# A fused attention, MLP and mixture-of-experts kernel: where the routing table's fill is kept, and when it is sent

## The chip, the cores and the metric

The kernel runs on one core of a Trainium2 chip. A core has TensorE (matmuls), VectorE, ScalarE, GpSimd and SyncE, which here issues nearly all DMAs from one queue, in order. The metric is device time in microseconds; three runs of the kernel before took 1059.51, 1066.27 and 1064.67 us, with a median of 1064.67.

## What is computed

Three layers, one behind the other, all in float32 at the interface:

```python
scores = scale * q @ k.T                              # 4 x 8 heads, 576 x 576, head dimension 64
kth = the 32nd largest of each row; others are masked
attn = softmax(masked scores); x = attn @ v           # 2304 tokens x 512
h = x @ w_in; g = relu(h) + log1p(exp(-abs(h)))       # 512 -> 2048
x = g @ w_out                                         # 2048 -> 512
e = argmax(x @ w_gate); out = gate * (relu(x @ w1[e]) @ w2[e])   # one of 8 experts a token
```

w_in and w_out arrive as 64-bit numbers, whose bits are decoded on the chip.

## The kernel before

Part one does attention, the dense layer and the routing; part two the experts. The program is recorded in Python in an order with priorities, and a scheduler that plays a timeline of its own sets the order on each engine from it. So an edit that moves one instruction in that timeline can reorder others far behind it.

Attention goes over 16 pairs of heads (four batches, four pairs each). `prep_split` loads nothing itself: it takes qn, kn and vn, which `load` (L323) fetched, splits each into two halves of 16 bits (ScalarE L370, then a subtraction L371, on VectorE for the first pair and on GpSimd for later ones) and issues transposing DMAs for k (L373, into kt) and q (L376, into q1), copies of q1 into q2 (L377, L378) and six small DMAs for v (L388 to L390). The tiles kt, q1 and q2 are of the pool kv, the first that part one opens. Score matmuls (L456) go in groups of two tiles, 72 groups in all; each is followed by an exact search of the 32nd largest on VectorE (L496 to L522), the exponentials on ScalarE (L530, L532) with subtractions on GpSimd (L531, L541, L542), a transposing DMA of the probabilities (L544), and, three groups later, the matmuls with v (L559).

`decode` turns one piece of w_in or w_out (128 x 512 numbers) into float32: a DMA into w (L238), ScalarE L247 and L251, VectorE L249 and L252, GpSimd L253. For w_in `decode_w_in` then makes the two halves w_in_s (ScalarE L258 and L259, GpSimd L260). Two pieces are decoded at the start, and up to four a group later.

Units of one or two finished tiles of x go through the dense layer: `unit_x` splits x (ScalarE L606, GpSimd L607), transposes it by DMA (L608), then 16 steps of `layer1` (L646, with w_in_s) and `layer2` (L686, with w_out_s). `route` writes each token's row to `rows` and its number to `table`, at the place of its expert (an indirect DMA on GpSimd, L755). Places of the table that no token takes have to hold the number TRASH. `clear_table` writes it everywhere at the start: a GpSimd iota of 128 x 146 numbers in SBUF (L128), and a DMA of them to the table (L129). Part two reads the table (L932).

The fill's tile comes from a pool `fill` of its own, opened and closed inside `clear_table`, ahead of part one's pools, which are allocated where it was. `w_out_s` is a tile of 128 x 16 x 512 numbers in the pool wp of part one; its last block of 512 columns is written by the last pieces decoded of w_out.

Of the kernel before, what the change touches and what calls it, by code (L numbers as in the profile page):

```python
# [11 lines left out]
I32 = mybir.dt.int32  # L12
# [8 lines left out]
NT, DM, DFF = 2304, 512, 2048  # L21
E, F2 = 8, 1024
# [3 lines left out]
KF = DFF // 128  # L26
KF2 = F2 // 128
SLOT = 256
# [7 lines left out]
TRASH = NT  # L36
# [58 lines left out]
def attn_moe_moe2(ctx, tc, q, k, v, w_in, w_out, w_gate, w1, w2, out):  # L95
    nc = tc.nc
# [11 lines left out]
                            fill=0.0, base=0, channel_multiplier=-1)  # L108
# [13 lines left out]
    table = dram.tile([E * NT + SLOT, 1], I32, name="table")  # L122
    rows = dram.tile([NT + 1, ROWW], F32, name="rows")

    def clear_table():
        with tc.tile_pool(name="fill", bufs=1) as p:
            fill = p.tile([128, (E * NT + SLOT) // 128], I32, name="fill")
            nc.gpsimd.iota(fill, pattern=[[0, (E * NT + SLOT) // 128]], base=TRASH, channel_multiplier=0)  # L128
            nc.sync.dma_start(table.rearrange("(p a) o -> p (a o)", p=128), fill)  # L129

    zrow = const.tile([27, 19], F32, name="zrow")
    nc.vector.memset(zrow, 0.0)
    nc.sync.dma_start(rows[TRASH:TRASH + 1, :].rearrange("o (p a) -> (o p) a", a=19), zrow)
# [2 lines left out]
    for i in range(2):  # L136
        h = ids[64 * i:64 * i + 64]
        nc.gpsimd.iota(h[:, :4 * B].rearrange("p (b t) -> p b t", t=4), pattern=[[S, B], [2, 4]], base=i,
                       channel_multiplier=R)
# [36 lines left out]

    def run(halves):
        nc.vector.memset(done, 0.0)
        clear_table()
        with ExitStack() as p:  # L180
            late = part_one(tc, p, q, k, v, w_in, w_out, const, ident, before, ones, iota_e, reg_e, wg, ids,
                            ohcum, done, early, table, rows, flags if halves else None, sums, w_sums, e_sums, kths)
        args = w1, w2, out, ident, ones, ohcum, done, early, late, table, rows, meta, left, rare
        with ExitStack() as p:
            part_two(tc, p, *args, (check, again) if halves else None, True)

        rv = nc.values_load(rare[0:1, 0:1], min_val=0, max_val=256)
        with tc.If(rv > 0):
            with ExitStack() as p:
                part_two(tc, p, *args, None, False)  # L190
            if halves:

                fv = nc.values_load(again[0:1, 0:1], min_val=0, max_val=128)
                with tc.If(fv > 0):
                    nc.vector.memset(ohcum, 0.0)
                    run(False)

    run(True)


def part_one(tc, ctx, q, k, v, w_in, w_out, const, ident, before, ones, iota_e, reg_e, wg, ids,
             ohcum, done, early, table, rows, flags, sums, w_sums, e_sums, kths):
    nc = tc.nc
# [24 lines left out]
    w_out_s = wp.tile([128, KF, DM], F32, name="w_out_s")  # L228
# [44 lines left out]
    def all_sum(bd, pool, tag):  # L273

        n = bd.shape[1]
        pb = pool.tile([128, 512], F32, name=tag)
        nc.tensor.matmul(pb[:, 0:n], lhsT=ones, rhs=bd, start=True, stop=True)
        bb = sm.tile([128, n], F32, name="bb" + tag)
        nc.vector.tensor_scalar(bb, pb[:, 0:n], 1e-30, None, op0=ALU.max)
        return bb  # L280

    w_inv = wp.tile([128, DFF // C], F32, name="w_inv")

    def split_w_in(j):
        bd = sm.tile([128, KD], F32, name="bdw")
        for kk in range(KD):
            t = dec.tile([128, C], F32, name="t")
            nc.scalar.activation(t, w_in_f[:, kk, j], AF.Abs, accum_out=bd[:, kk:kk + 1])
        bs = sm.tile([128, 1], F32, name="bs")
        nc.vector.tensor_reduce(bs, bd, op=ALU.add, axis=AX.X)  # L290
        up, down = pow2(all_sum(bs, ps_h, "h"), "h")
        nc.vector.tensor_scalar(w_inv[:, j:j + 1], down, 2.0 ** -8, None, op0=ALU.mult)
        for kk in range(KD):
            t = dec.tile([128, C], F32, name="t")
            nc.scalar.activation(t, w_in_f[:, kk, j], AF.Copy, scale=up)
            nc.scalar.activation(w_in_s[:, kk, j, 0], t, AF.Copy)
            nc.gpsimd.tensor_tensor(out=w_in_s[:, kk, j, 1], in0=t, in1=w_in_s[:, kk, j, 0], op=ALU.subtract)
# [11 lines left out]
    def decode_some(n):  # L309
        for _ in range(n):  # L310
            if dec_q:
                f, *a = dec_q.pop(0)
                f(*a)
# [12 lines left out]
    def prep_load(m):  # L326
        src = [None] * 3
        bd = sm.tile([128, 3], F32, name="bd") if flags is None else sums[:, m]
        pair[m] = (src, bd)
        for i in range(3):  # L330
            load(m, i)
        if flags is None:
            magnitudes(m, stg.tile([128, R * D], F16, name="st"))
# [6 lines left out]
    def prep_scale(m):  # L340
        b = pairs[m][0]
        src, bd = pair[m]
        if flags is not None:
            return
        up, iv = pow2(all_sum(bd, ps_m, "m"), "m")
        sc = sm.tile([128, 8], F32, name="sc", bufs=KVB + 2)
        nc.vector.tensor_copy(sc[:, 0:3], up)
        nc.vector.tensor_tensor(out=v_up[:, b:b + 1], in0=v_up[:, b:b + 1], in1=up[:, 2:3], op=ALU.min)
        nc.vector.scalar_tensor_tensor(sc[:, 3:4], iv[:, 0:1], 1.0 / D ** 0.5, iv[:, 1:2],
                                       op0=ALU.mult, op1=ALU.mult)  # L350
        nc.vector.tensor_scalar(sc[:, 4:5], sc[:, 3:4], -1.0, None, op0=ALU.mult)
        for i in (1, 0, 2):
            nc.scalar.activation(src[i], src[i], AF.Copy, scale=sc[:, i:i + 1])
        pair[m] = (*src, sc)
# [106 lines left out]
    def emit_scores(gi):  # L461
        s = row.tile([128, 2, S], F32, name="s")
        pa = ps_s.tile([128, 2, PS], F32, name="sa")
        for i, x in enumerate(groups[gi]):
            emit_qk(*x, pa[:, i], 0, 4)
        nc.scalar.activation(s[:, :, :PS], pa, AF.Copy)
        pb = ps_s.tile([128, 2, 512], F32, name="sb")
        for i, x in enumerate(groups[gi]):
            emit_qk(*x, pb[:, i, :PS + US], 4, R)
        if flags is None:  # L470
            nc.scalar.activation(s[:, :, PS:], pb[:, :, :PS + US], AF.Copy)
        sc_t[gi] = s, pb
# [224 lines left out]
    def some_work(k):  # L697
        for _ in range(k):
            moe_step()
            if side:  # L700
                next(side[0], None)
                if side[0].gi_frame is None:
                    side.pop(0)
# [144 lines left out]
    for i in range(-1, n + LAG):  # L848
        if i == -1:
            with tc.high_priority(offset=AHEAD):  # L850
                for m in range(RB):
                    prep_load(m)
                prep_scale(0)
        for m, step in steps.get(i, []):
            with tc.high_priority(offset=A_PREP):
                prep_step(m, step)
        while done_prep < whole and when[done_prep] <= i:
            with tc.high_priority(offset=A_PREP):
                if to_scale:
                    prep_scale(to_scale.pop()[0])  # L860
                prep_split(done_prep)
                if done_prep + RB < len(pairs):
                    prep_load(done_prep + RB)
                if done_prep + 1 < len(pairs):
                    to_scale.append((done_prep + 1, i + SCALE))
            done_prep += 1
        if to_scale and to_scale[0][1] <= i:
            with tc.high_priority(offset=AHEAD):
                prep_scale(to_scale.pop()[0])
        if i == -1:  # L870
            decode_some(2)
        if i + 1 < n:
            with tc.high_priority(offset=A_SC):
                emit_scores(i + 1)
        if 0 <= i < n:
            with tc.high_priority(offset=AHEAD):
                emit_softmax(i)
            with tc.high_priority(offset=0):
                decode_some(DECR)
        j = i - LAG  # L880
        if j >= 0:
            with tc.high_priority(offset=A_AV), ExitStack() as behind_scores:
                if i + 1 < n:

                    behind_scores.enter_context(tc.issue_after(last_qk[0].ins))
                for x in groups[j]:
                    emit_av(*x)
            for u in units.get(j, []):
                started += 1
                ready.append((u, started))  # L890
        if ready or cur or behind or side:
            credit += MOER
            some_work(int(credit))
            credit -= int(credit)
# [270 lines left out]
```

## Time and profile before

| | |
|---|---|
| three runs | 1059.51, 1066.27, 1064.67 us |
| the profiled execution, device time | 1059.72 us |
| its span in the profile | 1058.0 us |
| TensorE busy | 885.0 us, 84% |
| VectorE busy | 849.3 us, 80% |
| ScalarE busy | 801.2 us, 76% |
| GpSimd busy | 604.0 us, 57% |
| mean granted clock of TensorE | 0.936 of full speed |
| the hardware DMA queue's packets | 67.1% of 16 engines' span |

The span runs from the first to the last instruction of one execution; its device time is 1.7 us longer. Busy time is an average over stages with different limits: attention and the dense layer run interleaved up to about 740 us, the experts behind that. An engine's idle time costs something only where others wait for it, so a stage is read by what its engines waited for.

### The profile page before, as it was taken

Reading aid. Unit: us, or ns where it says so; the run is one execution under the profiler, and the core shown is the slowest. Engines: PE = TensorE matmul, PEld = TensorE weight load, DVE = VectorE, ACT = ScalarE, POOL = GpSimd, SP = SyncE. Lnnn points to the kernel's source line nnn. Section 1 sums busy time; section 2 is a strip of 40 time slices with the busy share of each in tenths; the row PEclk is TensorE's granted clock in tenths of the full one; section 3 lists DMA queues with packets and bytes.
Section 4 is the critical chain, followed back from the end, with each engine's and each line's share of the span. In section 5 each row is a group of like instructions: output and inputs, shape, how many; then the busy total and the mean of one; then the engine's idle time right before and its main releaser. Section 6 shows DMA issues by size and latency. Waiting matters only on the chain.

```text
span 1058.0 us, 22206 instructions
## 1 busy us (share of the span) xinstructions
PE 885.0 (84%) x7146; PEld 655.0 (62%) x7146; DVE 849.3 (80%) x3021; ACT 801.2 (76%) x1866; POOL 604.0 (57%) x631
## 2 busy tenths in 40 slices
PE   1124359774998989998999999999999999999994
PEld 0013236443675656675666666676787989999993
DVE  4779999998997968996989999955356987777773
ACT  5878898988888979987998888863678555555552
POOL 3888898998767768876778777652001022111111
PEclk9986559876999989998999999999999999999998
DMA  7897799788799987669978855464301667666650
GB/s 188 193 205 189 180 192 193 179 168 172 114 131 164 138 152 129 117 80 150 152 131 120 99 90 95 72 86 131 102 12 31 170 220 243 242 212 230 237 202 23
DMA packets 295859, 156.97 MB, mean 148 GB/s; under 512 B 257524, under 2 KB 257652, under 8 KB 295732
## 3 DMA queue, kind: packets, MB, share of 16 engines
q1 hardware_dynamic: 292116, 145.73, 67.1%
q0 software_dynamic: 3616, 9.72, 2.6%
q8 instruction: 58, 0.95, 0.4%
q14 instruction: 69, 0.57, 0.2%
HBM read 77.89 MB, written 11.11 MB: 84 GB/s over the span
## 4 chain that ended last, share of the span: by engine, by line
PE 47%; DVE 13%; DMA 12%; ACT 9%; POOL 8%; issue 6%; SPq 4%; POOLq 0%; ACTq 0%; DVEq 0%
PE h L646 11%; PE h L996 9%; PE y L686 8%; PE y L1009 8%; PE y L683 3%; DVE mx L522 3%; DVE wk L518 3%; DMA xT<-xh 3%; POOL e L531 2%; POOL p L542 2%; DMA w<-in_moe_w_in_dram 2%; PE sb L456 2%; PE m L559 1%; ACT e L532 1%; PE sa L456 1%
## 5 line engine op out<-in xcount | busy, mean ns | idle before, releaser
L646 PE MATMUL h<-xT,w_in_s 128*128 128x256 f16 (+1 forms) x1920 | 228.7, 269 | 22.9 <-ACT sa L660 14.4
L686 PE MATMUL y<-w_out_s,g 128*128 128x512 f32 x480 | 229.0, 601 | 1.3 <-ACT g L661 1.2
L646 PEld LDWEIGHTS <-w_in_s 128*128 128x128 f16 x1920 | 174.9, 101 | 82.7 <-issue 52.7
L531 POOL TENSOR_TENSOR e<-s,e 128x576 f32<-128x576 f32 x144 | 204.0, 1432 | 17.7 <-ACT e L530 10.4
L522 DVE MAX8 mx<-wk 128x8 f32<-128x128 f32 (+2 forms) x432 | 200.9, 503 | 0.1
L542 POOL TENSOR_TENSOR p<-e,p 128x512 f16<-128x512 f32 x144 | 167.8, 1165 | 0.0
L456 PEld LDWEIGHTS <-q 128*128 128x128 f16 (+1 forms) x640 | 55.8, 108 | 175.4 <-issue 125.8
L518 DVE MATCH_REPLACE8 wk<-mx,wk 128x128 f32<-128x128 f32 (+1 forms) x432 | 145.1, 343 | 0.1
L686 PEld LDWEIGHTS y<-w_out_s,g 128*128 128x128 f32 x480 | 82.7, 192 | 64.0 <-issue 58.1
L976 POOL DMA_INDIRECT out_dram<-ot,idx x19 | 19.5, 1028 | 176.1 <-DVE ot L975 173.4
L532 ACT ACTIVATE e<-e,bias 128x576 f32<-128x576 f32 x144 | 110.4, 768 | 12.7 <-POOL e L531 12.2
L996 PEld LDWEIGHTS h<-xT,wf 128*128 128x128 f32 x864 | 111.8, 191 | 5.4 <-ACT wf L957 0.2
L996 PE MATMUL h<-xT,wf 128*128 128x256 f32 x864 | 113.9, 283 | 0.0
L456 PE MATMUL sa<-kt,q 128*128 128x256 f16 (+1 forms) x320 | 54.0, 302 | 71.0 <-DMA kt<-st 23.4
L1009 PE MATMUL y<-wf,hT 128*128 128x512 f32 x432 | 112.8, 398 | 0.0
L456 PE MATMUL sb<-kt,q 128*128 128x320 f16 (+1 forms) x320 | 62.7, 338 | 53.6 <-ACT s L502 53.5
L530 ACT ACTIVATE e<-s,kths 128x576 f32<-128x576 f32 x144 | 104.9, 767 | 0.8
L559 PEld LDWEIGHTS <-pT 128*128 128x128 f16 (+1 forms) x1440 | 86.8, 106 | 22.9 <-issue 19.8
L559 PE MATMUL m<-v,pT 128*128 128x65 f16 (+1 forms) x1440 | 93.9, 201 | 7.2 <-DVE xtail L586 4.3
L540 ACT ACTIVATE p<-e 128x576 f16<-128x576 f32 x144 | 97.4, 678 | 0.7
L541 POOL TENSOR_TENSOR p<-e,p 128x64 f16<-128x64 f32 x144 | 46.1, 320 | 70.4 <-ACT p L540 65.9
L1009 PEld LDWEIGHTS y<-wf,hT 128*128 128x128 f32 x432 | 76.7, 189 | 13.0
(235 smaller groups left out, 1791.1 us busy)
## 6 DMA issues: line engine op xcount, KB each, us to landing
w1r<-in_moe_w_dram SPq DMA_DIRECT2D x20, 1024.0 KB, 6.3
w2r<-in_moe_w_dram SPq DMA_DIRECT2D x20, 1024.0 KB, 7.8
w<-in_moe_w_in_dram SPq DMA_DIRECT2D x16, 512.0 KB, 4.0
w<-in_moe_w_out_dram SPq DMA_DIRECT2D x16, 512.0 KB, 4.0
rows<-xr SPq DMA_DIRECT2D x37, 128.2 KB, 3.1
qn<-in_q_dram SPq DMA_DIRECT2D x16, 288.0 KB, 4.1
kn<-in_k_dram SPq DMA_DIRECT2D x16, 288.0 KB, 6.1
vn<-in_v_dram SPq DMA_DIRECT2D x16, 288.0 KB, 3.5
```

Source lines behind the costliest of these rows:

```text
L456: last_qk[0] = nc.tensor.matmul(ps[p0:p1], lhsT=qs[:, h, r0:r1, :].rearrange("p r d -> p (r d)"), rhs=kt[:, k0:k1, cs], start=first, stop= ...
L518: nc.vector.match_replace(out=to, in_to_replace=mx[:, i, 8 * j:8 * j + 8], in_values=src[i], imm_value=NEG)
L522: nc.vector.max(out=mx[:, i, 8 * j + 8:8 * j + 16], in_=src[i])
L530: nc.scalar.activation(e[i], s[i], AF.Relu, bias=kths[:, 2 * gi + i], scale=-K_UP)
L531: nc.gpsimd.tensor_tensor(out=e[i], in0=s[i], in1=e[i], op=ALU.subtract)
L532: nc.scalar.activation(e[i], e[i], AF.Exp, bias=bt[:, i], scale=SCORE)
L542: nc.gpsimd.tensor_tensor(out=p16[:, S + D:], in0=e[i][:, 0:S - D], in1=p16[:, 0:S - D], op=ALU.subtract)
L559: nc.tensor.matmul(o[:, h, 0:D + 1], lhsT=pT(r), rhs=v16[:, h, c, 0:D + 1], start=r == 0, stop=r == R - 1)
L646: nc.tensor.matmul(hps[:, :n], lhsT=w_in_s[:, c, j, p, o:o + 128], rhs=xT[:, 0:len(u.tiles), r, c, :], start=m == 0, stop=m == 3 * KD - 1)
L686: nc.tensor.matmul(u.y[i], lhsT=g[:, cs], rhs=w_out_s[:, f, :], start=f == 0, stop=f == KF - 1)
L996: nc.tensor.matmul(h, lhsT=w1f[:, a, c, :], rhs=xT[:, b, c, :], start=n == 0, stop=n == 3 * KD - 1)
L1009: nc.tensor.matmul(y[i], lhsT=hT[g][:, a, i * 128:i * 128 + 128], rhs=w2f[:, b, :], start=g == 0 and n == 0, stop=g == KF2 - 1 and n == 2)
```

## The change

The function `clear_table` moves into part one. Its tile is now the first 146 numbers of the last block of `w_out_s`, read as integers, and it is called behind the first pair's preparation and the first two decoded pieces, in place of the call ahead of part one. Nothing else is edited.

```diff
-    def clear_table():
-        with tc.tile_pool(name="fill", bufs=1) as p:
-            fill = p.tile([128, (E * NT + SLOT) // 128], I32, name="fill")
-            nc.gpsimd.iota(fill, pattern=[[0, (E * NT + SLOT) // 128]], base=TRASH, channel_multiplier=0)
-            nc.sync.dma_start(table.rearrange("(p a) o -> p (a o)", p=128), fill)
...
     def run(halves):
         nc.vector.memset(done, 0.0)
-        clear_table()
         with ExitStack() as p:
             late = part_one(tc, p, q, k, v, w_in, w_out, const, ident, before, ones, iota_e, reg_e, wg, ids,
...
+    def clear_table():
+        fill = w_out_s[:, KF - 1, :(E * NT + SLOT) // 128].bitcast(I32)
+        nc.gpsimd.iota(fill, pattern=[[0, (E * NT + SLOT) // 128]], base=TRASH, channel_multiplier=0)
+        nc.sync.dma_start(table.rearrange("(p a) o -> p (a o)", p=128), fill)
...
         if i == -1:
             decode_some(2)
+            clear_table()
         if i + 1 < n:
             with tc.high_priority(offset=A_SC):
                 emit_scores(i + 1)
```

The scheduler's order changes with it, on all engines. In the changed kernel line numbers up to here are 2 to 7 lower (L374 is what L376 was), and the numbers behind names differ. SP's queue near its start, before; q_170 is the first pair's q1, p_177 its split input, fill the table's fill:

```order
L133 DMA rows<-zrow 27x19
L129 DMA table<-fill 128x146
L238 DMA w<-in_moe_w_in_dram 128x1024 x2
L323 DMA qn<-in_q_dram 128x576
L376 DMA_TRANSPOSE q_170<-p_177 128x9x64
L373 DMA_TRANSPOSE kt<-st 128x9x128
L376 DMA_TRANSPOSE q_170<-p_177 128x9x64
L388 DMA v_184<-vs 64x5x130
L377 DMA q_171<-q_170 64x1152
```

And now, q_163 being the first pair's q1:

```order
L127 DMA rows<-zrow 27x19
L231 DMA w<-in_moe_w_in_dram 128x1024 x2
L278 DMA table<-w_out_s 128x146
L374 DMA_TRANSPOSE q_163<-p_170 128x9x64
L371 DMA_TRANSPOSE kt<-st 128x9x128
L374 DMA_TRANSPOSE q_163<-p_170 128x9x64
L386 DMA v_177<-vs 64x5x130
L375 DMA q_164<-q_163 64x1152
```

The table's DMA went behind the two loads of w_in, and a load of qn (of the second pair) is gone from here. SP's queue a little further on, from the first pair's copy of q, before (q_205 is the second pair's q1; the loads of qn, kn and vn are the third pair's and the second pair's):

```order
L378 DMA q_171<-q_170 64x1152
L376 DMA_TRANSPOSE q_205<-p_215 128x9x64 x2
L389 DMA v_184<-vs 64x4x130
L390 DMA v_184<-vs 64x130
L388 DMA v_184<-vs 64x5x130
L389 DMA v_184<-vs 64x4x130
L390 DMA v_184<-vs 64x130
L323 DMA qn<-in_q_dram 128x576
L323 DMA kn<-in_k_dram 128x576
L323 DMA vn<-in_v_dram 128x576
L238 DMA w<-in_moe_w_in_dram 128x1024 x2
L377 DMA q_206<-q_205 64x1152
```

And now, where q_198 is the second pair's q1 and the three loads are all the second pair's:

```order
L376 DMA q_164<-q_163 64x1152
L387 DMA v_177<-vs 64x4x130
L388 DMA v_177<-vs 64x130
L386 DMA v_177<-vs 64x5x130
L387 DMA v_177<-vs 64x4x130
L388 DMA v_177<-vs 64x130
L321 DMA qn<-in_q_dram 128x576
L321 DMA kn<-in_k_dram 128x576
L321 DMA vn<-in_v_dram 128x576
L231 DMA w<-in_moe_w_in_dram 128x1024 x2
L374 DMA_TRANSPOSE q_198<-p_208 128x9x64 x2
L371 DMA_TRANSPOSE kt<-st 128x9x128
```

The second pair's two transposes of q went behind the loads of kn, vn and w_in. GpSimd's queue at the first unit's split of x (x_778), before:

```order
L253 TENSOR_TENSOR w_out_s<-xr,w 128x512
L419 TENSOR_TENSOR st<-qn,st 128x9x64
L531 TENSOR_TENSOR e<-s,e 128x576 x2
L607 TENSOR_TENSOR xh<-x_778,xh 128x512
L253 TENSOR_TENSOR t<-xr,w 128x512
```

And now, the same tile being x_773:

```order
L539 TENSOR_TENSOR p_1333<-e,p_1333 128x64
L540 TENSOR_TENSOR p_1333<-e,p_1333 128x512
L417 TENSOR_TENSOR st<-qn,st 128x9x64
L605 TENSOR_TENSOR xh<-x_773,xh 128x512
L529 TENSOR_TENSOR e<-s,e 128x576 x2
```

The split of x went ahead of the two subtractions of the group's softmax.

## Rows read from the trace of the kernel before

**Rows 1.** The page: span; engine, busy us, share, instructions.
```profile
span 1058.0 us, 22206 instructions
PE 885.0 (84%) x7146; PEld 655.0 (62%) x7146; DVE 849.3 (80%) x3021; ACT 801.2 (76%) x1866; POOL 604.0 (57%) x631
```

**Rows 2.** Stretches: length, busy us of each engine (instructions), clock, DMA share, GB/s.
```profile
0.00:60.00 60.00, 9.50 (x34) 4.27 (x34) 39.39 (x127) 42.67 (x87) 36.55 (x49) 1.00 0.83 195
...
200.00:300.00 100.00, 71.01 (x641) 48.04 (x640) 93.20 (x335) 88.04 (x194) 87.58 (x91) 0.80 0.85 154
...
500.00:600.00 100.00, 97.96 (x894) 66.91 (x893) 93.30 (x383) 90.34 (x217) 78.40 (x85) 1.00 0.87 129
...
900.00:1000.00 100.00, 100.00 (x652) 91.29 (x651) 71.03 (x119) 56.54 (x112) 15.94 (x16) 1.00 0.64 223
```

**Rows 3.** Timeline of SP's queue: start us, us, line, operation, out<-in, count.
```profile
3.20 0.37 SPq L129 DMA_DIRECT2D table<-fill  x1
3.61 0.93 SPq L238 DMA_DIRECT2D w<-in_moe_w_in_dram  x2
...
7.43 1.34 SPq L376 DMA_TRANSPOSE q<-p  x1
8.87 1.87 SPq L373 DMA_TRANSPOSE kt<-st  x1
10.79 1.28 SPq L376 DMA_TRANSPOSE q<-p  x1
...
14.07 0.49 SPq L377 DMA_DIRECT2D q<-q  x1
...
15.29 2.59 SPq L376 DMA_TRANSPOSE q<-p  x2
...
21.88 0.42 SPq L323 DMA_DIRECT2D kn<-in_k_dram  x1
...
22.87 0.85 SPq L238 DMA_DIRECT2D w<-in_moe_w_in_dram  x2
```

**Rows 4.** Waits of SP's queue, 0 to 50 us: total us, times, longest.
```profile
SPq L376 <- DMA table<-fill: 1.9, 1, 1.9
```

**Rows 5.** Timeline of VectorE; in brackets idle time before, and its releaser.
```profile
4.35 0.76 DVE L371 TENSOR_TENSOR p<-qn,p 128x576 f16<-128x576 f32 x1 [2.45 <-ACT p L370]
...
30.55 0.70 DVE L249 TENSOR_SCALAR y<-y 128x512 uint32<-128x512 uint32 x1 [1.97 <-ACT y L247]
...
36.74 0.43 DVE L496 TENSOR_TENSOR sb<-sb,s 128x256 f32<-128x256 f32 x1 [0.37 <-ACT s L466]
```

**Rows 6.** Timeline of ScalarE: two reads of loaded pieces of w_in.
```profile
9.41 0.62 ACT L247 ACTIVATE y<-w 128x512 f32<-128x512 f32 x1 [1.95 <-DMA w<-in_moe_w_in_dram]
...
29.90 0.62 ACT L247 ACTIVATE y<-w 128x512 f32<-128x512 f32 x1 [2.05 <-DMA w<-in_moe_w_in_dram]
```

**Rows 7.** Timeline of TensorE: first scores of the first and second pair.
```profile
13.36 0.37 PE L456 MATMUL sa<-kt,q 128*128 128x256 f16 x1 [13.36 <-DMA kt<-st]
...
33.59 1.01 PE L456 MATMUL sa<-kt,q 128*128 128x256 f16 x4 [10.09 <-DMA kt<-st]
```

**Rows 8.** Stretches of one microsecond, columns as in rows 2.
```profile
8.00:9.00 1.00, 0.00 (x0) 0.00 (x0) 0.00 (x0) 0.00 (x0) 0.00 (x0) 1.00 0.93 363
```

**Rows 9.** The chain that ended last: start us, us, what (second unit's x).
```profile
261.64 3.09 DMA xT<-xh
```

**Rows 10.** All instructions of line L530: duration min/median/max ns, first and last start.
```profile
L530 ACT ACTIVATE e<-s,kths x144: 757/763/801, 32.2 to 699.4; 128x576 f32<-128x576 f32 x144
```

**Rows 11.** Waits, 200 to 220 us, on decoded pieces of w_in.
```profile
PEld L646 <- ACT w_in_s L259: 7.0, 2, 4.9
PE h L646 <- ACT w_in_s L259: 6.4, 2, 4.4
```

**Rows 12.** Timeline of GpSimd at the first unit's split of x.
```profile
143.48 1.59 POOL L531 TENSOR_TENSOR e<-s,e 128x576 f32<-128x576 f32 x1
145.04 1.60 POOL L607 TENSOR_TENSOR xh<-x,xh 128x512 f16<-128x512 f32 x1
```

## The prediction

> **What bounds the kernel now.** I read four views in this order: the table of stretches, the timelines of the first 40 us engine by engine, the list of SP's waits, and the chain of work that ended last. The page gives a span of 1058.0 us and TensorE busy for 885.0 us of it [rows 1]. The stretches show where its 173 idle us lie [rows 2]: in the first 60 us TensorE works 9.5 us, from 200 to 300 us it works 71.0 of 100, from 500 to 600 it works 98.0, from 900 to 1000 it works 100. So the kernel has two regimes. Up to some 260 us attention sets the pace: from 200 to 300 us VectorE is busy 93 of 100 us and ScalarE and GpSimd 88 each. Behind that TensorE is the bound, and its work is the same before and after. What the change can do is to bring the second regime forward or push it back, and whatever it moves there should reach the end.
>
> The change touches the first microseconds. The timeline of SP shows its DMAs there [rows 3]: table<-fill at 3.20, two loads of w_in from 3.61, then the first transpose, of q, at 7.43. VectorE had that transpose's input ready at 4.35 + 0.76 = 5.11 [rows 5], yet SP stood still for 1.9 us, and the list of its waits names table<-fill as the releaser [rows 4]. The transposed tile is the first one of the pool that was opened where the fill's pool had been closed, so it takes over the fill's bytes and has to wait until the DMA that reads them has landed. Everything of the first pair stands behind that transpose in SP's queue: kt at 8.87, the second half of q at 10.79, the copy of q at 14.07 [rows 3]; TensorE's first matmul follows at 13.36, released by kt [rows 7].
>
> **The change part by part.** (1) The fill moves to the last columns of w_out's place. GpSimd's iota keeps its place in the order and its size. The bytes that it borrows are decoded into only at the end of the weights, long after the table has been written, and the first scatter into the table needs a routed unit; so the new place adds a wait that nothing reaches. Price nothing; the cover is the whole of part one's first two sweeps.
>
> (2) The wait of the first transpose goes. In the changed order SP issues the two loads of w_in, then the table, then the transpose. The issues take 0.93 and 0.37 us [rows 3], so 3.20 + 0.93 + 0.37 is 4.5, and the transpose then waits for VectorE alone, to 5.11. It starts 7.43 - 5.11 = 2.3 us earlier. kt's input is the next VectorE row, so kt and the second half of q can follow back to back as they do now, and with them the scores of the first pair. The bound above is 2.3 us. The bound below is nothing: the transposes are now issued while two pieces of w_in are still under way. ScalarE got the first of it at 9.41, having waited for it 1.95 us [rows 6], and from 8 to 9 us the DMA engines moved 363 GB/s with a share of 0.93 [rows 8], so there is no free room for transposes before some 9 us. I take 2.3 of it, since kt, the late one, was issued at 8.87 and landed at 13.36: there is room behind 9.4 us that the three transposes can fill more densely than one after the other from 7.43 to 12.07.
>
> The Trainium skill (DMA: Bandwidth & Descriptors, section Queues, rings and completion order) speaks against this step: SP has one row of rings, and on each DMA engine descriptors are consumed in ring order, so a transpose behind the loads of w_in is served after them. No row of this case separates the service of a transpose from its landing; by that rule alone the step would give what the first rival below gives.
>
> (3) The second pair's loads move in SP's queue, since the schedule is made anew. Before, qn of the second pair was issued ahead of the first transpose and its two transposes stood at 15.29 for 2.59 us, ahead of kn at 21.88 and w_in at 22.87 [rows 3]. Now kn and w_in stand ahead of these two transposes, and qn behind the first pair's work. kn is therefore issued 2.6 + 2.3 = 4.9 us earlier, at 17.0, and w_in at 18.0. Before, the way from kn's issue to the second pair's scores on TensorE took 33.59 - 21.88 = 11.7 us [rows 3, 7]. Now the two transposes of 2.6 us fall into that way, so the scores come at 17.0 + 11.7 + 2.6 = 31.3, again 2.3 us earlier. The earlier w_in has an effect of its own: ScalarE waited 2.05 us for that load at 29.90 and VectorE 1.97 us behind it [rows 5, 6], and these waits can go, which would make it 2.3 + 2.0 = 4.3 us on VectorE. But at 36.74 VectorE already waited 0.37 us for the second pair's scores [rows 5], so what it gains there it waits for here. In the sum this is nothing; the bounds are nothing and 2.0 us.
>
> (4) The order behind that differs in many places. At the first unit GpSimd now splits its x ahead of the next group's two subtractions, the second of which took 1.59 us right before it [rows 12]; the unit can start some 3.2 us earlier. That is hidden, since TensorE is not the bound there: the second unit's x was transposed only at 261.64 [rows 9]. The decoding of weights is put off by up to a group against the softmax and meets it again by the second unit: the work up to there is the same, and its price is nothing while TensorE idles 29 of 100 us [rows 2].
>
> The sum: 2.3 + 0 + 0 = 2.3 us less. Against the profiled execution, 1059.72 us, that is 1057.4. The three runs shown have a median of 1064.67 and reach from 1059.51 to 1066.27, so the profiled one is a fast one; the mean of the four is 1062.5, and against that I forecast 1060 us.
>
> **Rivals.** *The transposes wait in the DMA engines instead.* They are issued early and served late, so the change does not do what it says: no gain, 1062.5 us. For it speaks the full share at 8 to 9 us [rows 8]; against it that the new order has one load less ahead of the transposes, the second pair's qn.
>
> *The new order gains a group.* Attention goes ahead of decoding. 144 rows of the softmax's first step, two a group, lie between 32.2 and 699.4 us [rows 10], so a group takes 667 / 71 = 9.4 us. If unit two starts one group earlier and TensorE then stays full, the gain is 9.4 + 2.3 = 11.7, 1051 us. Against it: the second unit's split moves by less than a group in GpSimd's order, and the decoding has been made up by then.
>
> *The late decoding holds up TensorE, and the kernel gets slower.* TensorE already waited for the last decoded parts of w_in, 6.4 us and its weight loads 7.0 us between 200 and 220 us [rows 11]; in the new order the first unit's last four steps stand one group later. TensorE works its queue in order, so scores behind these steps come late, VectorE starves, and one group is lost: 9.4 - 2.3 = 7.1 us more, 1069.6 us. It decides when that wait grows past the idle time around it, that is when the last matmuls of the first unit push the scores behind them by more than the 2.3 us won. Against it: the second unit could not begin before 261.64 + 3.1 [rows 9], so the first has from 220 to 264.7 us, some 45 us, to end.
>
> **How the numbers follow.** I give the forecast 0.45, the first rival 0.20, the second 0.20, the third 0.15. What a measurement of this kernel can tell from no change is about 1%, 10.6 us. Only the second rival comes to it, and just so: faster by over 1% 0.16, half of that rival and 0.06 of the spread of the others. Slower by over 1% 0.09: 0.05 for the third rival with a second group lost, and the spread of the others. Within 1%: 0.75. The range leaves out the far halves of the second and third rivals: 1050 to 1069 us. For the likeliest case alone it is 1056 to 1063: 4.3 to no gain, and the scatter of the runs.
>
> **What would show it.** In the changed profile SP's first transpose should start at 5.1 to 5.3 us and no longer be released by a DMA of the table; TensorE's first matmul should come at 11 us and the second pair's scores at 31. If the first matmul is still at 13, the DMA engines held it. If unit two's x is transposed at 252, the second rival is right; if the wait for w_in of rows 11 doubles and the unit's x comes after 262, the third. The forecast is wrong if the second regime begins at another time by more than 5 us, or if TensorE's idle time behind 300 us changes.

## The result

The changed kernel takes 1067.42 us (median of 20 runs, 1062.07 to 1072.5), the kernel before 1060.12 (20 runs, 1053.61 to 1066.27): a ratio of 1.0058, 95% interval 1.0041 to 1.0074. It is slower by 0.6%, some 6 us by the ratio and 7.3 us by the medians, where 2.5 us less was forecast. The profiled execution took 1062.07 us and is the fastest of its twenty, so a second profile of the same kernel, with 1074.82 us, stands beside it below.

The page of the kernel after, and its stretches, answer [rows 1, 2]:

```profile
span 1060.4 us, 22234 instructions
PE 884.7 (83%) x7146; PEld 653.7 (62%) x7146; DVE 854.3 (81%) x3021; ACT 801.3 (76%) x1866; POOL 603.8 (57%) x631
```

```profile
0.00:60.00 60.00, 9.89 (x37) 4.60 (x38) 40.97 (x130) 46.08 (x96) 39.85 (x52) 1.00 0.84 201
200.00:300.00 100.00, 72.28 (x639) 48.06 (x638) 92.75 (x331) 86.80 (x193) 88.44 (x89) 0.77 0.76 150
500.00:600.00 100.00, 97.33 (x854) 65.43 (x853) 90.19 (x367) 87.64 (x208) 75.95 (x82) 0.99 0.81 129
```

TensorE's work is the same 885 us; it does more of it by 60 and by 300 us, and less from 500 to 600. At the start the lead that was forecast is there, in part smaller and in part larger. SP's timeline, answering [rows 3]:

```profile
3.21 0.83 SPq L231 DMA_DIRECT2D w<-in_moe_w_in_dram  x2
4.09 0.43 SPq L278 DMA_DIRECT2D table<-w_out_s  x1
5.17 1.33 SPq L374 DMA_TRANSPOSE q<-p  x1
6.61 2.55 SPq L371 DMA_TRANSPOSE kt<-st  x1
...
17.61 0.42 SPq L321 DMA_DIRECT2D kn<-in_k_dram  x1
```

TensorE's first scores of both pairs, answering [rows 7]:

```profile
11.75 0.37 PE L454 MATMUL sa<-kt,q 128*128 128x256 f16 x1 [11.75 <-DMA kt<-st]
...
29.11 0.37 PE L454 MATMUL sa<-kt,q 128*128 128x256 f16 x1 [5.85 <-DMA kt<-st]
```

The first transpose starts at 5.17 instead of 7.43, the first matmul at 11.75 instead of 13.36, the second pair's scores at 29.11 instead of 33.59. The wait for decoded parts of w_in did not grow: 6.5 us on the weight loads from 100 to 260 us, against 7.0 before.

```profile
PEld L644 <- ACT w_in_s L252: 6.5, 3, 3.1
```

The second unit's x, in the chain that ended last, is at 259.56 instead of 261.64 [rows 9]. The same chain holds the row on which the result turns:

```profile
259.56 3.67 DMA xT<-xh
...
485.74 9.28 DMA xT<-xh
```

To see where the lead goes, take the dense layer's steps (ScalarE's `sa<-h`, L658, 160 of them) and compare when the same step starts. In before the 1st is at 152.9, the 17th at 267.5, the 65th at 462.1, the 81st at 534.8, the 153rd at 802.9 us. The table gives the difference to before in the profiles of all kernels below; the last column is what is lost from the 65th to the 81st.

```
us against before         1st   17th   65th   81st  153rd   65th to 81st
after                    -4.8   -1.5   -3.3   +2.3   +2.4   +5.6
change_again             -3.8   +2.3   +3.9  +12.6  +13.4   +8.8
old_place_new_order      -1.6   +2.7   +2.6   +8.3   +9.5   +5.7
old_to_125               -3.9   -1.0   -1.7   +3.9   +4.9   +5.6
old_to_430               +0.2   +1.1   +1.1   +7.5   +7.6   +6.3
new_order_copy_first     -2.6   +0.5   +1.4   +4.5   +3.9   +3.0
new_order_split_later    -4.7   -2.5   -3.8   +0.1   +1.1   +3.8
new_order_old_decode     +5.0  +11.9  +10.2  +14.2  +15.0   +3.9
old_order_copy_behind    -0.9   +0.1   -0.4   +2.4   +1.5   +2.7
new_place_old_order      -1.2   -1.3   -2.5   -2.3   -3.1   +0.2
new_to_125               +3.1   +4.5   +6.4   +6.4   +4.2    0.0
new_to_250               -4.4   +0.6   -1.3   -1.5   -3.5   -0.3
old_to_510               -0.5   +0.9   +2.0   +2.6   +2.7   +0.6
old_order_split_later    -1.3   -1.6   -2.7   -4.8    0.0   -2.1
old_order_decode_8_later +1.9  +31.6  +31.3  +30.7  +29.9   -0.6
```

In its first profile the kernel after is still 3.3 us ahead at 462 us, and 2.3 behind at 535. Two profiles of one kernel scatter: change_again is the same kernel, is 3.9 us behind at 462 us already, and loses 8.8 where after loses 5.6. So a single entry is good to some us, and the last column says more than the others. Whatever has the new order there, and the order before with one row of it moved (old_order_copy_behind), loses 2.7 to 8.8 us in that stretch; all others with the order before lose 0.6 at most. The experiments follow this from the outside in.

### The profile page after: what moved, and what is told of

Its sections match the earlier page's. It is cut to its first block, busy times and chain, and to the rows that moved or that the text cites. A ratio compares the mean times of both kernels' runs of the same rounds, so it can differ in the third digit from the quotient of the medians.

```text
span 1060.4 us, 22234 instructions
## 1 busy us (share of the span) xinstructions
PE 884.7 (83%) x7146; PEld 653.7 (62%) x7146; DVE 854.3 (81%) x3021; ACT 801.3 (76%) x1866; POOL 603.8 (57%) x631
## 4 chain that ended last, share of the span: by engine, by line
PE 47%; DVE 21%; DMA 11%; ACT 9%; POOL 5%; issue 4%; SPq 2%; POOLq 0%; DVEq 0%; ACTq 0%
PE h L995 10%; PE y L1008 9%; PE h L644 9%; PE y L684 8%; DVE mx L520 5%; DVE wk L516 5%; PE y L681 3%; DMA w<-in_moe_w_in_dram 2%; DMA kt<-st 2%; DMA xT<-xh 2%; DVE wk L499 2%; PE m L557 1%; DMA qn<-in_q_dram 1%; PE sb L454 1%; POOL p L540 1%
## 5 line engine op out<-in xcount | busy, mean ns | idle before, releaser
L644 PE MATMUL h<-xT,w_in_s 128*128 128x256 f16 (+1 forms) x1920 | 226.5, 268 | 16.9 <-ACT w_in_s L252 5.6
L644 PEld LDWEIGHTS <-w_in_s 128*128 128x128 f16 x1920 | 173.3, 100 | 80.7 <-issue 49.7
L454 PEld LDWEIGHTS <-q 128*128 128x128 f16 (+1 forms) x640 | 54.5, 107 | 180.6 <-issue 122.2
L530 ACT ACTIVATE e<-e,bias 128x576 f32<-128x576 f32 x144 | 110.6, 768 | 9.4 <-POOL e L529 8.9
L454 PE MATMUL sb<-kt,q 128*128 128x320 f16 (+1 forms) x320 | 62.8, 338 | 65.5 <-ACT s L500 65.3
L454 PE MATMUL sa<-kt,q 128*128 128x256 f16 (+1 forms) x320 | 51.9, 297 | 65.8 <-ACT s L464 21.9
```

The lines of the kernel that those rows point to most:

```text
L454: last_qk[0] = nc.tensor.matmul(ps[p0:p1], lhsT=qs[:, h, r0:r1, :].rearrange("p r d -> p (r d)"), rhs=kt[:, k0:k1, cs], start=first, stop= ...
L530: nc.scalar.activation(e[i], e[i], AF.Exp, bias=bt[:, i], scale=SCORE)
L644: nc.tensor.matmul(hps[:, :n], lhsT=w_in_s[:, c, j, p, o:o + 128], rhs=xT[:, 0:len(u.tiles), r, c, :], start=m == 0, stop=m == 3 * KD - 1)
```

## Experiments: the place or the order

An edit in a scheduled program does two things, what it says and a new order. To part them, the order of each engine was written out as a table of ranks and pinned, with an edge without a semaphore between neighbours; so any order can be had with either place of the fill. In the pinned kernels line numbers are some 320 higher (L927 is L604 of after, L823 is L500, L777 is L454, L967 is L644, L981 is L658).

```diff
+        for a, b in zip(queue, queue[1:]):
+            tc.add_manual_dep(b, a.name, mybir.DependencyInfo(mybir.DependencyClass.NoSync,
+                                                              mybir.DependencyReason.DATA), reason="pin")
...
             part_two(tc, p, *args, (check, again) if halves else None, True)
+        if halves:
+            pin(tc, FILL)
```

**new_place_old_order**: the fill in w_out_s, the order of before on every engine.

> The change (fill in w_out's place, no pool of its own), but every engine's instructions of both parts pinned, by edges that only order, to the order they have in the kernel before; the table's DMA stands ahead of the two loads of w_in as before. So of the change only the lost wait is left. Theory 1 (the new order costs what the lost wait gains and more): first transpose at 5.1 us, and 2 to 4 us faster than before, ratio 0.996 to 0.998. Rival A (the fill's new place or the earlier transposes themselves cost, whatever the order): as slow as the change, +6 us, ratio 1.006. Rival B (the lead at the start goes nowhere, the order does all): no difference, ratio 0.999 to 1.001.

Measured: 1057.92 against 1059.9 us, ratio 0.9994 (0.9972 to 1.0016).

**old_place_new_order**: the fill in its own pool, the order of after.

> The kernel before (fill in a pool of its own, its bytes taken over by the first transposed tile), but pinned to the order that the changed kernel has on every engine, the table's DMA behind the two loads of w_in. So of the change only the order is left, and the first transpose still waits for the table's DMA, some 2 to 4 us. Theory 1: slower than the changed kernel by what the wait costs, +8 to +10 us against before, ratio 1.008 to 1.010. Rival A: the order costs nothing, within 2 us of before, ratio 0.999 to 1.002. Rival B: as slow as the change, +6 us, ratio 1.006.

Measured: 1068.11 us, ratio 1.0083 (1.0053 to 1.0112).

**change_again**: the kernel after once more, on the same chip as these two.

> The changed kernel itself, on the chip of the other two, so that they can be set against it as well as against the kernel before. All theories: +6 us against before, ratio 1.004 to 1.008.

Measured: 1069.03 us, ratio 1.0075 (1.0046 to 1.0105).

The order costs the 0.6 to 0.8%; the place is worth nothing that these runs can tell, as rival B of both expectations had it. That holds although the place does what it should. With the fill in its pool and the new order the first transpose waits 4.9 us for the table, as SP's waits from 0 to 20 us show, and starts at 9.54 instead of 5.17; the median is the same as change_again's within 1 us. The one is pinned and the other is not, so the pins cost nothing that shows either.

```profile
SPq L699 <- DMA table<-fill: 4.9, 1, 4.9
```

In the old order the lost wait buys nothing even at the start. SP's timeline of new_place_old_order, and TensorE's first matmul:

```profile
3.62 0.90 SPq L553 DMA_DIRECT2D w<-in_moe_w_in_dram  x2
5.19 0.33 SPq L644 DMA_DIRECT2D qn<-in_q_dram  x1
5.56 2.25 SPq L697 DMA_TRANSPOSE q<-p  x1
7.92 2.93 SPq L694 DMA_TRANSPOSE kt<-st  x1
```

```profile
13.54 0.37 PE L777 MATMUL sa<-kt,q 128*128 128x256 f16 x1 [13.54 <-DMA kt<-st]
```

The transposes are issued 1.87 and 0.95 us earlier than before and take 2.25 and 2.93 us to issue, where [rows 3] have 1.34 and 1.87; kt lands no earlier. Here it goes as the first rival has it: the transposes are issued early, behind two loads of w_in and one of qn, and served late. In the new order, with qn's load gone from there, 1.6 us remain of the 2.3. The Trainium skill (DMA: Bandwidth & Descriptors, section Queues, rings and completion order) states that each DMA engine consumes descriptors in the order of the ring. The landing of kt agrees with it: issued 0.95 us earlier, it let the first matmul start at 13.54, where before had 13.36. No run takes the loads away, so that they are what holds the transposes is not shown by itself.

## Experiments: which part of the order

The decoding of weights was the part that the prediction had in mind. Two kernels move it alone: the new order with the decoding's instructions where before has them against the softmax groups, and the old order with the decoding's instructions on SP, ScalarE, VectorE and GpSimd put 8 us later from 60 us on.

**new_order_old_decode**

> The change with its own order pinned, but the instructions of the 32 decoded pieces of w_in and w_out (their DMAs and their work on ScalarE, VectorE and GpSimd) put where they stand against the attention groups in the kernel before, that is 2 to 14 us, mostly some 8 us, earlier than in the change. TensorE keeps the new order. Theory 2 (the new order is slow because the decoding is put off behind the attention of the first 125 us and then falls together with the first unit): most of the loss goes, ratio 0.998 to 1.002 against before. Rival C (the order of attention, the first unit and TensorE's queue is what costs; the decoding only comes along): still slow, 1.006 to 1.009.

Measured: 1080.0 against 1059.97 us, ratio 1.0204 (1.0173 to 1.0235).

**old_order_decode_8_later**

> The fill in its new place and the order of the kernel before, but the instructions of the decoded pieces that ran from 60 us on are put 8 us later against all others on SP, ScalarE, VectorE and GpSimd (26 of 32 pieces). Nothing else moves. Theory 2: the loss comes back, ratio 1.005 to 1.009. Rival C: as the old order, 0.998 to 1.002.

Measured: 1091.54 us, ratio 1.0313 (1.028 to 1.0346).

Neither cures nor copies the loss; both make a new and larger one. The second is the third rival of the prediction, made on purpose: TensorE's waits from 100 to 260 us have 19.4 us for decoded parts of w_in, three times the 6.4 of before, and the table shows 31.6 us lost at the 17th step. The wait grew by 13.0 us; the rest of the 31.6 was not followed. So that mechanism exists and has a price, but the change did not set it off.

```profile
PE h L967 <- ACT w_in_s L574: 19.4, 4, 8.6
```

Orders were then cut in time: what started before the border in one order, the rest in the other.

**new_to_250** (new order first, old behind 250 us) and **old_to_125** (the reverse, at 125 us)

> The fill in its new place; the instructions that the changed kernel started before 250 us of its trace in the new order, all later ones in the order of the kernel before. Theory 2 and rival C: the loss arises up to 250 us, so it is all there, ratio 1.005 to 1.009. Rival D (the later order, up to the end of the dense layer, costs as much): about half, 1.002 to 1.004, or none.

Measured: 1059.36 against 1059.97 us, ratio 1.0003 (0.998 to 1.0025).

> The reverse cut, earlier: the instructions that the kernel before started before 125 us in the old order, all later ones in the new order, the fill in its new place. By 125 us the old order has decoded 16 pieces, the new one 14 or 15. Theory 2: the backlog is what costs, so nearly all of the loss is gone, ratio 0.998 to 1.002. Rival C: what costs is the new order around the first unit, behind 125 us, so it is still there, 1.005 to 1.009. Rival D: 1.002 to 1.005.

Measured: 1065.52 us, ratio 1.0061 (1.0038 to 1.0084).

The loss stays with the later part of the order. Of all that starts behind 250 us the prediction costed the second unit's x alone.

**old_to_430** and **old_to_510**

> The fill in its new place, the order of before for what started before 430 us there, the order of the change behind it. If the loss lies behind 430 us (theory A with what comes later): ratio 1.004 to 1.008. If it lies between 250 and 430 us (where the order of the change keeps the DMA engines less busy, a share of 0.70 against 0.86 to 0.89 from 250 to 300 us): ratio 0.999 to 1.002.

Measured: 1066.06 against 1060.56 us, ratio 1.0043 (1.0016 to 1.0071).

> The same with the border at 510 us, so that the place where ScalarE's copy stands behind the split is in the order of before. Theory A: most of the loss gone, ratio 1.000 to 1.003, and 3 to 4 us less than with the border at 430 us. If the loss comes from the order behind 510 us (part two's steps among the last groups): the same ratio as with the border at 430 us, 1.004 to 1.008. If the loss lay before 430 us: both 0.999 to 1.001.

Measured: 1059.74 us, ratio 0.9986 (0.9963 to 1.0009).

Some 6 us, nearly the whole loss, depend on the order between 430 and 510 us, and the intervals do not meet. **new_to_125** asked whether the early lead can reach the end.

> The order of the change for what started before 125 us there, the order of before behind it; the fill in its new place. At 124 us the new order is 4 us ahead, its lost wait and its later decoding together. If a lead there reaches the end: ratio 0.996 to 0.998. If it is given back where the weights that were not decoded must be (the prediction's part 4 and its third rival): no lead left at 250 us, ratio 0.999 to 1.002.

Measured: 1060.3 against 1058.8 us, ratio 1.001 (0.999 to 1.003). No lead reached the end, and the table shows none at the first step (3.1 us behind): the border itself made a wait, with scores that stood up to 8.1 us behind ScalarE's copies between 100 and 260 us, so this run says little about a lead.

## Experiments: one split on ScalarE

Between 430 and 510 us one pause of TensorE stands out. Its waits from 430 to 500 us, in after and then in new_place_old_order:

```profile
PE sb L454 <- ACT s L500: 6.1, 1, 6.1
```

```profile
PE h L967 <- ACT sa L981: 2.5, 1, 2.5
```

ScalarE's timeline at that place, in after:

```profile
488.56 0.20 ACT L658 ACTIVATION_READ_ACCUMULATOR sa<-h 128x1 f32 x1
495.11 0.63 ACT L604 ACTIVATE xh<-x 128x512 f16<-128x512 f32 x1 [6.35 <-DMA xT<-xh]
495.64 0.69 ACT L500 ACTIVATE s<-sb 128x640 f32<-128x640 f32 x1
```

And in new_place_old_order:

```profile
484.36 0.68 ACT L823 ACTIVATE s<-sb 128x640 f32<-128x640 f32 x1
484.95 0.19 ACT L829 ACTIVATE bias<-mx 128x2 f32<-128x2 f32 x1
491.20 0.63 ACT L927 ACTIVATE xh<-x 128x512 f16<-128x512 f32 x1 [6.06 <-DMA xT<-xh]
```

The split `xh<-x` of a unit's second tile has only one buffer and waits until the transposing DMA of the first tile has read it. That DMA takes 9.28 us here and 8.84 in new_place_old_order (`482.28 8.84 DMA xT<-xh` in its chain), where the second unit's took 3.67, and 3.09 before [rows 9]. Both orders have this wait of 6 us. What differs is what stands behind it in ScalarE's queue: in the old order a step of the dense layer, in the new one the copy of the scores out of PSUM, for which TensorE's next scores wait. And behind the pause TensorE's clock is low for a while. The stretches of 4 us, after and then new_place_old_order (third column from the right: granted clock):

```profile
488.00:492.00 4.00, 2.28 (x14) 1.27 (x14) 3.97 (x15) 0.76 (x3) 3.83 (x3) 1.00 0.99 27
492.00:496.00 4.00, 0.00 (x0) 0.00 (x0) 0.13 (x1) 0.90 (x2) 0.19 (x1) 0.86 1.33 202
496.00:500.00 4.00, 3.62 (x33) 2.51 (x33) 0.62 (x4) 4.00 (x13) 1.90 (x3) 0.50 0.81 193
500.00:504.00 4.00, 4.00 (x18) 2.16 (x17) 3.86 (x18) 3.40 (x8) 3.25 (x5) 0.79 1.00 169
```

```profile
492.00:496.00 4.00, 3.76 (x15) 2.54 (x15) 0.19 (x1) 3.97 (x12) 2.65 (x4) 0.60 1.15 170
496.00:500.00 4.00, 4.00 (x37) 2.42 (x37) 3.95 (x19) 4.00 (x10) 3.98 (x4) 1.00 0.77 114
```

After the pause the clock is at 0.50, that is 1.2 of 2.4 GHz, until past 500 us in after, and back at 1.00 by 496 us in the old order. Counted from where TensorE works again, the granted clock falls short of full by 4 x (0.50 + 0.21) = 2.8 us in after and by 4 x 0.40 = 1.6 us in the other. With the pause that makes (6.1 - 2.5) + (2.8 - 1.6) = 4.8 us, near the 5.4 us that part these two kernels in the last column of the table (5.6 - 0.2).

Against the kernel before itself, from which the table counts, the clock explains nothing. Its pause at this place; then the whole way from the 65th to the 81st step and the stretch from where TensorE works again, all in before; then the whole way in after:

```profile
PE h L646 <- ACT sa L660: 3.1, 1, 3.1
```

```profile
462.06:534.78 72.72, 69.61 (x600) 45.61 (x599) 60.64 (x245) 62.62 (x153) 53.49 (x58) 0.95 0.92 137
494.20:500.00 5.80, 5.79 (x17) 2.96 (x17) 2.17 (x9) 5.80 (x15) 4.45 (x5) 0.52 0.93 134
```

```profile
458.75:537.10 78.35, 71.18 (x611) 46.66 (x610) 64.03 (x257) 64.43 (x156) 56.51 (x61) 0.96 0.79 127
```

Behind a pause of 3.1 us the clock falls short by 5.8 x 0.48 = 2.8 us there, as much as behind the 6.1 us of after; behind a pause of 4.5 us in new_order_copy_first it is 4 x (0.34 + 0.09) = 1.7. So the low clock does not grow with the pause, and what sets its length is not shown. Of the 5.6 us against before, 4.1 are idle time of TensorE (7.2 against 3.1 between the two steps), 3.0 of them this pause; the other 1.5 are more busy time between these steps, which no run follows further.

Four kernels test the pause, each with one or two rows of ScalarE moved.

**new_order_copy_first**: the new order, the copy and the bias ahead of the split. ScalarE's order:

```diff
+s<-sb
+bias<-mx
 xh<-x
-s<-sb
 sa<-h
-bias<-mx
```

> Whole order of the change, with two rows moved on ScalarE alone: for one group, the copy of the second score tile (s<-sb) and the bias stand ahead of the split xh<-x of a unit, as in the order before, and no longer behind it. In the profile of the change this xh waits 6.3 us for a transpose of the unit's x at 495.1 us, the copy behind it waits with it, and TensorE stands 6.1 us for that copy (about 490 to 496); with the order before it stands 2.5 us there. Theory A (this pair of rows holds the scores up and is the larger part of the loss): TensorE's pause there falls to 2.5 us, some 4 us less, so about 1064 us where the change has 1068, ratio 1.004. Rival B (the loss is spread over many places; what is won here is lost to the next wait): the pause falls, but the time stays at 1067 to 1069, ratio 1.007 to 1.008. Rival C (the pause moves to another place in the chain): no less TensorE idle time between 430 and 520 us than in the change.

Measured: 1063.93 against 1060.56 us, ratio 1.0031 (1.0007 to 1.0055).

**old_order_copy_behind**: the old order, the split ahead of the copy.

```diff
+xh<-x
 s<-sb
 bias<-mx
-xh<-x
 sa<-h
```

> The reverse in one place: the fill in its new place with the whole order of before, but on ScalarE the split xh<-x of that unit stands ahead of this group's copy s<-sb and bias. Theory A: TensorE's pause at about 490 us grows from 2.5 to 6 us, so 3 to 4 us more than the 1059 us of the whole old order: 1062 to 1063, ratio 1.003. Rival B (spread): within 1 us of the whole old order, ratio 0.999 to 1.001. Rival C: a pause of 6 us, but made up behind it, since TensorE is not full before 600 us; ratio 1.000.

Measured: 1061.35 us, ratio 1.0017 (0.9989 to 1.0046).

**new_order_split_later** and **old_order_split_later**: the split behind the eight, or six, rows that followed it, down to a `p<-e`.

> Whole order of the change, but on ScalarE the waiting split xh<-x of that one unit stands behind the eight rows that follow it (the copy of the scores, the bias, three sa and g of the unit's steps, e, p), so that nothing of these waits for the transpose of the x before. If the pause of TensorE at 490 to 496 us (6.3 us, and 6.8 us at the lower granted clock behind it) is the larger part of what the new order loses: the pause shrinks to under 2 us, and 5 to 7 us are won against 1068, so 1061 to 1063, ratio 1.001 to 1.003. Rival (the loss is spread, and the pause comes back at the next row that needs the unit's x or at the next transpose): 1065 to 1068, ratio 1.004 to 1.007.

Measured: 1061.67 against 1058.8 us, ratio 1.0014 (0.9995 to 1.0033).

> The same in the whole order of before with the fill in its new place: the split behind the six rows that follow it there, down to p. The order before has a pause too, 2.5 us and 3.4 us at the lower clock. If that pause costs what it shows: 2.5 + 1.7 us less than the whole old order, ratio 0.995 to 0.997, faster than both kernels. Rival (what is won there is lost to the next wait, as with the copy put first): 0.999 to 1.000.

Measured: 1057.5 us, ratio 0.997 (0.9947 to 0.9993).

In either order the time falls as the split goes back in the queue: 1.0058 and 1.0075, then 1.0031, then 1.0014 in the new one; 1.0017, 0.9994, 0.997 in the old one. Neighbours' intervals overlap; those of the two ends don't in the new order, and overlap by 0.0004 in the old. The waits of TensorE from 430 to 520 us show what the rows did, in old_order_copy_behind, new_order_copy_first, new_order_split_later and old_order_split_later:

```profile
PE sb L777 <- ACT s L823: 5.2, 1, 5.2
PE h L967 <- ACT sa L981: 1.9, 1, 1.9
```

```profile
PE y L1007 <- ACT g L982: 4.8, 2, 4.5
```

```profile
PE h L967 <- ACT sa L981: 5.0, 2, 4.5
```

```profile
PE sa L777 <- ACT s L787: 1.1, 1, 1.1
PE sb L777 <- ACT s L823: 1.0, 1, 1.0
```

In the old order's waits the effect is whole: put behind, the copy makes TensorE wait 5.2 us for it; with the split later no wait over 1.1 us is left, and the table shows 2.1 us won there. In the new order the pause only changes its name. With the copy first TensorE stands 4.5 us for `g` of a step, which still is behind the split. With the split later it stands 4.5 us again, and now ScalarE waits for another transpose, that of q, as its timeline shows:

```profile
489.39 0.68 ACT L738 ACTIVATE w<-vn 128x576 f16<-128x576 f32 x1 [4.27 <-DMA q<-w]
...
497.65 0.62 ACT L927 ACTIVATE xh<-x 128x512 f16<-128x512 f32 x1
```

So at this place the transposes that are on the way land late, and a row of ScalarE that waits for one holds up all rows behind it. The place of split and copy is worth 2.4 us (0.9994 to 1.0017) to 4.7 us (1.0075 to 1.0031), about half of the loss; the intervals overlap at each of these steps, so its size is an estimate from medians. The kernel of the new order with the split later ended with less time than its pause of 4.5 us would let expect, so length of the pause in one profile and median are not the same thing. With the copy at the same place in both orders, the new one is still 4 to 6 us slower (1.0031 against 0.9994, 1.0058 and 1.0075 against 1.0017). That other part lies in the same stretch, by old_to_430 and old_to_510, and has no name.

What makes the transposes late is open as well. It shows in before, after, change_again, new_place_old_order and new_order_split_later, each time close behind the seventh scatter into the table (482.2 us in before, 481.1 in after). It is not the only such place: in before the transpose of x issued at 586.25, behind the ninth scatter (583.8), took 8.3 us to land, while in old_to_125 the one issued at 597.49, 11 us behind its ninth scatter (586.0), took 3.0:

```profile
xT<-xh SPq DMA_TRANSPOSE x1, 8.3
xT<-xh SPq DMA_TRANSPOSE x1, 3.0
```

That speaks for the scatter or what is sent with it, but no run moves a scatter. Another buffer for the split was not tried either.

## Why the prediction was wrong

- **(1), the fill's new place costs nothing: right.** Place and order taken apart, the place moves the median by 2 us less (new_place_old_order, with an interval that holds no change) or by 1 us more (change_again against old_place_new_order).
- **(2), the transposes 2.3 us earlier: right in kind, 1.6 us in size.** The first transpose came at 5.17, inside the forecast 5.1 to 5.3; the first matmul at 11.75 rather than 11, since kt's issue took 2.55 us. The first rival's delay fits the missing 0.7 us, and the whole of it in the old order.
- **(3), the second pair: more than forecast.** Its scores came at 29.11 instead of the 31.3 of the sum. kn was issued at 17.61, and the way from there took 11.5 us (11.7 before), not 14.3: the 2.6 us of the two transposes did not add to it. ScalarE's wait for the load of w_in, whose end was put at nothing, shrank from 2.05 to 0.75 us.
- **The second regime began when it should, within the scatter.** The second unit's x was transposed 2.1 us earlier, and the dense layer was 3.3 us ahead at 462 us in the same profile; in the second profile of the kernel it was 3.9 behind. So the sum of 2.3 us holds in one profile of two, and a lead of that size is not shown. Neither the second nor the third rival came about.
- **(4) is the step that failed: "its price is nothing while TensorE idles 29 of 100 us".** The cover named there ends at 300 us, and the reorder does not. The price was asked only up to the second unit; 5.6 us (8.8 in the second profile) were lost between 462 and 535 us, and by medians the order between 430 and 510 us alone costs 6.0 us. A pause has no cover there: from 500 to 600 us TensorE is busy 98 of 100 [rows 2]. The prediction said that a change of TensorE's idle time behind 300 us would make it wrong, and gave no chance to it. About half of the price is a row of ScalarE that waits for a transpose ahead of a copy; where the rest arises in that stretch stays open.
- **The rivals were all about the front of the program.** None was a wait behind 300 us that the new order sets up differently. The chain that ended last before has a row that named the place, beside the one in [rows 9]:

```profile
483.90 9.18 DMA xT<-xh
```

One transpose three times as long as its sister, on the chain, with ScalarE waiting for it: a place where the order of two rows is worth several us. That the range of 1050 to 1069 holds the median is luck: the arm that reaches there came from the third rival, and the time came from something else.

## What to carry to other kernels

Where a scheduler makes the order, a small edit is two changes, and only one of them is in the diff: compare the two orders through the whole program, and price a reorder at the longest waits of each engine, not only near the edit. Before taking such a result as the verdict on the idea, pin the order of before and run the edit alone; here the idea is worth nothing that can be told and the new order costs 0.6%. A buffer with one copy, whose writer stands in an engine's queue ahead of work that others need, is a price that depends on the order: put the row that may wait behind the rows that must not.

## What was not expected of the hardware

- A transposing DMA took 8.84 to 9.28 us close behind the seventh scatter, and 8.3 behind the ninth in before, against 3.09 for the same shape elsewhere, while the DMA engines had a busy share of 0.99 and moved 27 GB/s (488 to 492 us in after).
- The issue of a transpose is not of fixed length: among the first ones it took 1.28 to 1.34 us, but also 1.87, 2.25, 2.55 and 2.93 us. Loads of w_in were issued just ahead of short ones too (1.33 at 5.17 in after), so what sets it is not shown.
- What TensorE lost at the lower clock behind a pause did not go by its length: 2.8 us behind 6.1 us (after) and behind 3.1 us (before), 1.7 behind 4.5 us (new_order_copy_first), 1.6 behind 2.5 us (new_place_old_order).
- Orders in which only the decoding was moved were the slowest kernels of all, 1.0204 and 1.0313, with the same instructions on every engine.
